# Casting the first key and query halves on the chip, with the mask built in two parts, in a block-sparse attention and feed-forward kernel

## The chip, the core and the metric

The kernel runs on one core of a Trainium2 chip. The metric is the device time of one execution in microseconds, as the median of several runs. The engines are TensorE (PE, matrix products; PEld is its weight load), VectorE (DVE), ScalarE (ACT), GpSimd (POOL) and SyncE (SP, which here only issues transfers). The transfers themselves are done by 16 DMA engines.

## The reference

Attention over 4 batches, 8 heads, 768 positions and 64 columns per head, in blocks of 32 positions. A query block sees its neighbours, the first and the last block, and three sampled blocks. The first and the last query block see everything. The result of all heads, 512 columns per position, goes through a normalisation and a feed-forward layer with 2048 hidden columns, and is added to what went in.

```python
scores = scale * np.matmul(q, k.transpose(0, 1, 3, 2))
mask = np.abs(blk_i - blk_j) <= window
mask = mask | (blk_i == 0) | (blk_j == 0) | (blk_i == n_blocks - 1) | (blk_j == n_blocks - 1)
for qb in range(n_blocks):
    for kb in sampled_blocks[qb]:
        mask[qb * block:(qb + 1) * block, kb * block:(kb + 1) * block] = True
scores = np.where(mask, scores, -1000000000.0)
attn = np.exp(scores - np.max(scores, axis=-1, keepdims=True))
attn = attn / (np.sum(attn, axis=-1, keepdims=True) + 1e-09)
x = np.matmul(attn, v)          # all heads side by side
xn = (x - mu) / np.sqrt(var + 1e-06) * g_ln
out = x + np.maximum(xn @ w_ch1, 0.0) @ w_ch2
```

## The kernel before

**Units, segments, slots.** A unit is a batch and a third of its positions (256 rows); there are 12. A unit has four segments, one for each pair of heads, and a segment four slots: two tiles of 128 rows by two heads, 192 slots in all. The first eight segments, two units, are called early.

**Split numbers.** Products of float32 numbers are made from float16 halves: for queries, keys, values and weights a high half is the cast of the number, and a low half the difference between the number and its high half. A score is three products, high by high, high by low and low by high (`scores`, L467 to L475), summed in a `ps` buffer. There are two such buffers, so the pair of slots that comes next needs the buffers of the pair before.

**A slot's way.** DVE reads the scores with the mask added and writes them with their maximum (`masked_max`, L478, L484). ACT takes the exponential (L498). In an early slot PE turns the result in 128x128 pieces with an identity matrix (L512), DVE and ACT copy the pieces out (L519), and PE multiplies with the values (`pa`, L588). Later slots write float16 halves (L549, L553) and are turned by a DMA on SP's queue (L559, L562). When a unit's four segments are done, `layer_norm` (L629) makes the normalised rows xh and xl (L731, L735), and `ffn` (L740) runs the two feed-forward products (L754, L835).

**Weights.** They arrive in 64 bits a number. Three DVE steps (L423, L427, L431), two ACT steps (L458, L460) and a POOL subtraction (L461) make float16 halves of each chunk: eight chunks of W1, sixteen of W2. This runs beside the first units' attention.

**Keys and queries before.** `loads_k` (L284) loads a float32 key by SP's queue (`raw`, L292; two buffers, each free when the low half has been made), and loads the same key a second time by POOL's queue with a cast to float16 on the way (`kh`, L299). The low half `kl` (L295) is made by DVE for the first key, by POOL for all others. `loads_q` (L305) does likewise for queries (`qr` L313, `qh` L317, `ql` L320).

**The mask.** `build_mask` (L254) makes `allow` from the host's fixed part and the sampled blocks: a conversion (L255), three compares (L259) with a maximum each (L262), and a scaling (L263), over all six tiles of 128 rows at once. The fixed part is fetched first, the sampled blocks second, both on ACT's queue (L235, L237).

**What sets the order.** All work is entered as tasks in a `Plan` (L26) with an engine, a cost, the tasks it comes after, a rank and the buffers it takes and gives. `run` (L92) steps through an assumed time: of the tasks that are ready it takes for each engine the one that could start first, or the lowest rank among near equals, and emits it. The result is a fixed order of instructions for each engine, which the engine works through in that order. Costs and due times only shape this order; on the chip an instruction waits for its data. The feed-forward matmuls have the rank 1e6: they fill PE's time when nothing else is ready. The mask has the rank -2000, and PE's tasks cost 1.9 times as much in the plan until it takes the array as warm.

## Time and profile before

| what | value |
|---|---|
| median of 3 runs | 816.51 us (814.61 to 822.39) |
| profiled execution, its time | 817.7 us |
| its span | 815.9 us |
| mean granted clock of PE | 0.987 |
| PE busy | 779.8 us, 96% |
| DVE busy | 610.9 us, 75% |
| ACT busy | 514.9 us, 63% |
| POOL busy | 173.9 us, 21% |

The span is what the profile covers; the time of the same execution is 1.8 us longer. A timeline row gives the start and the duration in us, the engine, the line, the operation with what it writes and reads, and in brackets how long the engine was idle before and what released it. A row of grouped instructions gives their count, the busy time, the mean duration in ns and the idle time in front of them. "SPq" and "ACTq" are the issuing of transfers; a landing is counted from the issue.

### The profile page before, as it was taken

To read this page: it belongs to the slowest core of one execution; us is meant where nothing else is said; L and a number is where in the kernel's file an instruction comes from. 1 tells how busy PE (TensorE), PEld (TensorE's weight loads), DVE (VectorE), ACT (ScalarE), POOL (GpSimd) and SP (SyncE) were. 2 spreads that over 40 slices of the span, in tenths; PEclk is the share of its full clock that TensorE was granted. 3 is DMA by queue.
4 is the path that set the end of the run, shared out by engine and by line. 5 is a ranking of instruction groups with operands and counts; after the bars stand their busy time and mean duration, and the time that the engine had idled before them with its cause. 6 is when DMAs were issued, how large, how long until landed. Compare 5 with 4: busy or idle time off the path is not lost.

```text
span 815.9 us, 18386 instructions
## 1 busy us (share of the span) xinstructions
PE 779.8 (96%) x7228; PEld 592.4 (73%) x7228; DVE 610.9 (75%) x1203; ACT 514.9 (63%) x942; POOL 173.9 (21%) x188
## 2 busy tenths in 40 slices
PE   4787899999999999999899999999999999999998
PEld 2454567777777867777677777777777777788887
DVE  5899988968988878868878778868869778745120
ACT  2778788668686666677666666668766656723020
POOL 4635454413211012143111012332100100000000
PEclk9799899999999999999999999999999999999999
DMA  9853424899989779999678699899697585750000
GB/s 283 289 174 95 132 70 116 159 159 207 168 155 141 130 136 168 160 193 173 124 136 141 107 152 174 168 181 169 131 144 142 107 150 101 115 107 2 27 2 27
DMA packets 293383, 112.49 MB, mean 138 GB/s; under 512 B 260400, under 2 KB 285104, under 8 KB 293296
## 3 DMA queue, kind: packets, MB, share of 16 engines
q1 hardware_dynamic: 283792, 104.91, 64.1%
q0 software_dynamic: 9216, 6.30, 6.2%
q8 instruction: 57, 0.93, 0.5%
q14 instruction: 30, 0.25, 0.1%
q10 hardware_dynamic: 288, 0.10, 0.1%
HBM read 48.34 MB, written 6.29 MB: 67 GB/s over the span
## 4 chain that ended last, share of the span: by engine, by line
PE 77%; DVE 11%; DMA 5%; ACT 4%; issue 1%; SPq 1%; ACTq 0%; DVEq 0%
PE bank L835 28%; PE bank L754 26%; PE ps L475 10%; PE pa L592 6%; DMA pt<-pl 3%; PE pa L597 3%; DVE p L484 2%; PE pa L588 2%; DVE pl L553 2%; PE bank L512 1%; ACT p L498 1%; DMA pt<-ph 1%; DVE w2h L427 1%; DMA samp_i<-sampled 1%; DMA raw<-w 1%
## 5 line engine op out<-in xcount | busy, mean ns | idle before, releaser
L498 ACT ACTIVATE p<-p,st 128x768 f32<-128x768 f32 x192 | 177.8, 926 | 43.4 <-DVE st L484 41.9
L549 ACT ACTIVATE ph<-p,st 128x768 f16<-128x768 f32 x160 | 145.3, 929 | 92.2 <-DVE st L540 42.0
L835 PE MATMUL bank<-hh,w2h 128*128 128x256 f16 x704 | 192.3, 273 | 2.5 <-DVE xc L685 2.5
L553 DVE SCALAR_TENSOR_TENSOR pl<-p,st,ph 128x768 f16<-128x768 f32 x160 | 164.3, 1038 | 38.9 <-DMA pt<-pl 37.4
L484 DVE CUSTOM_DVE_ANT_1 p<-ps,allow 128x768 f32<-128x768 f32 x192 | 178.4, 947 | 18.5 <-PE ps L475 17.4
L835 PE MATMUL bank<-hl,w2h 128*128 128x256 f16 x704 | 191.9, 273 | 0.0
L835 PE MATMUL bank<-hh,w2l 128*128 128x256 f16 x704 | 191.9, 273 | 0.0
L754 PEld LDWEIGHTS <-w1h 128*128 128x128 f16 x1536 | 146.9, 98 | 27.6 <-issue 10.7
L835 PEld LDWEIGHTS <-w2h 128*128 128x128 f16 x1408 | 134.5, 98 | 27.4 <-issue 12.4
L754 PE MATMUL bank<-xl,w1h 128*128 128x256 f16 x768 | 115.8, 274 | 0.0
L754 PE MATMUL bank<-xh,w1l 128*128 128x256 f16 x768 | 115.7, 273 | 0.0
L754 PE MATMUL bank<-xh,w1h 128*128 128x256 f16 x768 | 115.4, 273 | 0.1
L769 ACT ACTIVATE hh<-bank 128x512 f16<-128x512 f32 x96 | 56.6, 590 | 80.9 <-PE bank L754 80.2
L775 DVE SCALAR_TENSOR_TENSOR hl<-bank,hh 128x512 f16<-128x512 f32 x96 | 65.9, 686 | 35.4 <-ACT hh L769 35.1
L475 PE MATMUL ps<-kh,qh 64*128 64x256 f16 (+1 forms) x384 | 72.2, 338 | 14.2 <-DMA qh<-q 7.3
L592 PE MATMUL pa<-pt,vh 128*64 128x512 f16 x480 | 82.1, 383 | 0.7 <-issue 0.6
L754 PEld LDWEIGHTS <-w1l 128*128 128x128 f16 x768 | 73.9, 98 | 12.1 <-issue 3.8
L475 PEld LDWEIGHTS <-qh 64*128 64x128 f16 x768 | 32.5, 96 | 62.6 <-issue 28.2
L835 PEld LDWEIGHTS <-w2l 128*128 128x128 f16 x704 | 68.9, 98 | 8.0
L475 PE MATMUL ps<-kl,qh 64*128 64x256 f16 (+1 forms) x384 | 69.7, 334 | 1.4 <-DVE kl L295 1.4
L475 PE MATMUL ps<-kh,ql 64*128 64x256 f16 (+1 forms) x384 | 68.3, 334 | 1.2 <-DVE ql L320 1.2
L597 PE MATMUL pa<-pt,vl 128*64 128x256 f16 x480 | 67.4, 273 | 0.0
(106 smaller groups left out, 921.7 us busy)
## 6 DMA issues: line engine op xcount, KB each, us to landing
raw<-k SPq DMA_DIRECT2D x16, 384.0 KB, 4.6
qr<-q SPq DMA_DIRECT2D x48, 128.0 KB, 3.3
raw<-w SPq DMA_DIRECT2D x12, 512.0 KB, 3.6
out<-ot SPq DMA_DIRECT2D x48, 128.0 KB, 2.0
vr<-v SPq DMA_DIRECT2D x24, 192.0 KB, 2.9
w2l<-w SPq DMA_DIRECT2D x4, 1024.0 KB, 9.6
kh<-k POOLq DMA_DIRECT2D x16, 192.0 KB, 5.2
qh<-q POOLq DMA_DIRECT2D x48, 64.0 KB, 3.5
```

Of the source, the lines that this page charges most:

```text
L475: nc.tensor.matmul(s.ps[:, lo:hi], x[rows, s.qs], y[rows, lo:hi], start=n == 0, stop=n == len(terms) - 1)
L484: nc.vector.tensor_tensor_reduce(out=s.p.rearrange(blk, k=BLK), in0=s.ps[:, 0:S].rearrange(blk, k=BLK), in1=bias, scale=-0.125, scalar=3.0 ...
L498: nc.scalar.activation(s.p, s.p, AF.Exp, bias=s.st[:, j : j + 1], scale=-1.0, accum_out=total)
L549: nc.scalar.activation(s.ph, s.p, AF.Copy, scale=s.r)
L553: nc.vector.scalar_tensor_tensor(out=s.pl, in0=s.p, scalar=s.r, in1=s.ph, op0=ALU.mult, op1=ALU.subtract)
L588: nc.tensor.matmul(seg.pa[half[hh], 0:CH], vo.whole(hh)[:, t, :], pts[keys[hh]][:, t, :], start=t == 0, stop=t == KT - 1, skip_group_check ...
L592: nc.tensor.matmul(seg.pa[half[hh], 0 : 2 * CH], vo.vh[:, hh, t, :], pts[keys[hh]][:, t].rearrange("p i n -> p (i n)"), start=t == 0, stop ...
L597: nc.tensor.matmul(seg.pa[half[hh], 0:CH], vo.vl[:, hh, t, :], pts[keys[hh]][:, t, 0, :], start=False, stop=t == KT - 1, skip_group_check= ...
L754: nc.tensor.matmul(dst, w[:, ct, fs], x[:, ct, :], start=n == 0 and ct == 0, stop=n == 2 and ct == CT - 1, skip_group_check=True)
L769: nc.scalar.activation(u.hh[:, f : f + 2, :].rearrange("p f n -> p (f n)"), bank[plan.where("bank", own)], AF.Relu)
L775: nc.vector.scalar_tensor_tensor(out=u.hl[:, f : f + 2, :].rearrange("p f n -> p (f n)"), in0=bank[plan.where("bank", own)], scalar=0.0, i ...
L835: nc.tensor.matmul(dst, w[:, k, e * P : (e + 1) * P], x[:, k, :], start=k == 0 and n == 0, stop=k == FT - 1 and n == 2)
```

## The change

- **Casts.** The first four keys (`CASTK`) and the first four query loads (`CASTQ`) are no longer loaded a second time by POOL's queue. ACT casts the loaded float32 key or query; for the very first query DVE does. From the fifth on nothing changes.
- **Mask.** `build_mask(lo, hi)` makes the tiles from lo to hi. The first part has the two tiles of the first 256 positions (all that the first unit of a batch needs), the second the other four. A slot's maximum comes after its own part. Their ranks are 0 and 6, with 5400 and 12000 as the earliest planned times.
- **Fetch.** The sampled blocks are fetched ahead of the fixed part.
- **Planner.** The engines' planned times start at 700 and the transfers' at 1800 in place of 0. The array counts as warm when it was busy for over 0.85 of the last 3400 ns of planned time, and stays so down to 0.4. A `filler` of idle matmuls is defined, but called only for starts before `keep`, and `KEEP` is 0.

```diff
     def run(self):
-        clock = dict.fromkeys(("PE", "DVE", "ACT", "POOL", "SP"), 0.0)
+        clock = dict.fromkeys(("PE", "DVE", "ACT", "POOL", "SP"), 700.0)
-        bus, mode, done, warm, since = 0.0, None, 0, False, 0.0
+        bus, mode, done, warm = 1800.0, None, 0, False
...
-                    start = max([now] + [x.free if x.engine == "PE" == e or x.order == t.order
+                    start = max([t.wake] + [x.free if x.engine == "PE" == e or x.order == t.order
...
+            if t.engine == "PE" and start < self.keep:
+                self.fill(clock["PE"], start, 115 if warm else 220)
...
-                if start - clock["PE"] > self.idle:
-                    warm, since = False, start
-                warm = warm or start - since > self.heat
+                part = sum(max(0, b - max(a, start - self.span)) for a, b in self.work[-60:])
+                part /= self.span
+                warm = part > self.hot or warm and part > self.cold
...
+    KEEP = 0
+    CASTK, CASTQ = 4, 4
...
-    plan.idle, plan.heat, plan.deep = 2500.0, 4200.0, 7000.0
+    plan.span, plan.hot, plan.cold, plan.deep = 3400.0, 0.85, 0.4, 7000.0
+    plan.keep, plan.first = KEEP, 1400.0
...
-    nc.scalar.dma_start(allow, blocks)
     samp_i = const.tile([P, KT, 2 * NR], I32, name="samp_i")
     nc.scalar.dma_start(samp_i, sampled.bitcast(I32))
+    nc.scalar.dma_start(allow, blocks)
...
-    def build_mask():
-        nc.vector.tensor_copy(samp_f, samp_i.rearrange("p c (r t) -> p c r t", t=2)[:, :, :, 0])
+    def build_mask(lo, hi):
+        ts, n = slice(lo, hi), hi - lo
+        nc.vector.tensor_copy(samp_f[:, ts],
+                              samp_i.rearrange("p c (r t) -> p c r t", t=2)[:, ts, :, 0])
...
-        o.high = plan.add("POOL", 560, lambda: nc.gpsimd.dma_start(o.kh, ks[b, pr]), (o.raw,),
-                          rank, 2300, load=1100, order="k")
+        if idx < CASTK:
+            o.high = plan.add("ACT", 900, lambda: nc.scalar.copy(o.kh, o.kr), (o.raw,), rank)
+        else:
+            o.high = plan.add("POOL", 560, lambda: nc.gpsimd.dma_start(o.kh, ks[b, pr]),
+                              (o.raw,), rank, 2300, load=1100, order="k")
...
-        e, c = ("POOL", 660) if n else ("DVE", 650)
+        if n < CASTQ:
+            o.high = plan.add("ACT" if n else "DVE", 310 if n else 200, lambda: (
+                nc.scalar.copy if n else nc.vector.tensor_copy)(o.qh, o.qr), (o.raw,), rank)
...
+        e, c = ("POOL", 660) if n else ("DVE", 350)
...
-    mask = plan.add("DVE", 2300, build_mask, (), -2000, 100)
-    mask.more = 4000
+    masks = [plan.add("DVE", 1250, lambda: build_mask(0, TS), (), 0, 100),
+             plan.add("DVE", 2100, lambda: build_mask(TS, KT), (), 6, 100)]
+    masks[0].wake, masks[1].wake = 5400.0, 12000.0
...
-                last_m = plan.add("DVE", 880, lambda s=s: masked_max(s), (sc, mask, last_m),
+                last_m = plan.add("DVE", 880, lambda s=s: masked_max(s), (sc, masks[u.c > 0], last_m),
```

The lines of the program move by 18 to 36 places: the masked maximum is L519 after the change, the W1 and W2 steps on DVE are L458, L462 and L466.

**DVE at the program's start, up to the second masked maximum** (L484, ISA; `qh`, `ql`, `kl` are halves of the first query and key, `allow` is the mask). Before, from the conversion of the sampled blocks on, the compares and maxima shown once:

```order
L255 CAST samp_f<-samp_i 128x18
L259 TENSOR_TENSOR w1h<-allow,samp_f 128x144
L262 TENSOR_TENSOR allow<-allow,w1h 128x144
...
L263 TENSOR_SCALAR allow<-allow 128x144
L295 TENSOR_TENSOR kl_138<-raw_119,kh_137 128x768
L320 TENSOR_TENSOR ql_121<-qr_142,qh_141 128x256
L484 ISA p_192,st_193<-ps_174,allow 128x768
```

After, the halves stand ahead of the mask, and the mask has 48 columns in place of 144; behind the second maximum come the three steps of the first W1 chunk, which stood behind the third before:

```order
L349 CAST qh_132<-qr_133 128x256
L355 TENSOR_TENSOR ql_121<-qr_133,qh_132 128x256
L323 TENSOR_TENSOR kl_130<-raw_119,kh_129 128x768
L281 CAST samp_f<-samp_i 128x6
L287 TENSOR_TENSOR w1h<-allow,samp_f 128x48
L290 TENSOR_TENSOR allow<-allow,w1h 128x48
...
L291 TENSOR_SCALAR allow<-allow 128x48
L519 ISA p_191,st_192<-ps_169,allow 128x768
...
L458 TENSOR_SCALAR w2h<-w1r_156 128x1024
L462 SCALAR_TENSOR_TENSOR w2h<-w1r_156,w2h 128x1024
```

**DVE further on, between the fourth and the fifth masked maximum** (p_257 is the fourth before, p_250 after; w1r is a W1 chunk as loaded, `nm` the sums of the exponentials). Before:

```order
L484 ISA p_257,st_223<-ps_203,allow 128x768
L484 ISA st_223 128x1
L423 TENSOR_SCALAR w2h<-w1r_172 128x1024
L427 SCALAR_TENSOR_TENSOR w2h<-w1r_172,w2h 128x1024
L919 TENSOR_SCALAR nm_199<-nm_199 128x4
L920 RECIPROCAL nm_199<-nm_199 128x4
L484 ISA p_290,st_291<-ps_265,allow 128x768
```

After, the second part of the mask stands here, and the sums and the second step of the chunk come behind the fifth maximum. Up to the instruction that writes the first unit's xl, the order after has 22 masked maxima in place of 23, 20 copies in place of 22, and one W2 step less:

```order
L519 ISA p_250,st_240<-ps_201,allow 128x768
L519 ISA st_240 128x1
L554 COPY pt_1_247<-bank_101 128x2x128
L458 TENSOR_SCALAR w2h<-w1r_159 128x1024
L281 CAST samp_f<-samp_i 128x12
L287 TENSOR_TENSOR w1h<-allow,samp_f 128x96
L290 TENSOR_TENSOR allow<-allow,w1h 128x96
...
L291 TENSOR_SCALAR allow<-allow 128x96
L519 ISA p_293,st_294<-ps_254,allow 128x768
```

**ACT at the program's start** (L498 and L533 are exponentials, L519 and L554 copies of turned pieces, L458 and L493, L460 and L495 the two steps of a W chunk). Before:

```order
L498 ACTIVATE p_192,nm_199<-p_192,st_193 128x768
L498 ACTIVATE p_197,nm_199<-p_197,st_193 128x768
L519 COPY pt_0_232<-bank_101 128x4x128
L498 ACTIVATE p_222,nm_199<-p_222,st_223 128x768
L519 COPY pt_1_240<-bank_103 128x4x128
```

After, four casts stand in front of the first exponential, and the cast of the third key (kh_183) stands ahead of the second step of the first W1 chunk and of the third exponential; that of the fourth key follows seven instructions later:

```order
L328 CAST kh_129<-raw_119 128x768
L328 CAST kh_135<-raw_120 128x768
L349 CAST qh_138<-qr_139 128x256
L349 CAST qh_141<-qr_142 128x256
L533 ACTIVATE p_191,nm_198<-p_191,st_192 128x768
L533 ACTIVATE p_196,nm_198<-p_196,st_192 128x768
L554 COPY pt_0_230<-bank_101 128x4x128
L493 ACTIVATE w2h<-w2h 128x1024
L554 COPY pt_1_247<-bank_103 128x4x128
L328 CAST kh_183<-raw_119 128x768
L495 CAST w1h<-w2h 128x4x256
L533 ACTIVATE p_239,nm_198<-p_239,st_240 128x768
```

On PE, 132 transposes of 128x128 stand ahead of the first feed-forward matmul in place of 138, and otherwise the same instructions; the 2304 + 2304 feed-forward matmuls and all other counts are as before. On POOL the eight casting loads are gone. SP issues the same loads; the value load that stood ahead of the first W1 chunk now stands further back.

More of the change, by code (lines that the diff above doesn't have):

```diff
@@ L36, in __init__ @@
     def __init__(self):
-        self.tasks, self.rings, self.sets = [], {}, {}
+        self.tasks, self.rings, self.sets, self.work = [], {}, {}, []
     def ring(self, name, size):
@@ L49, in add @@
                             after=[x for x in after if x is not None], end=None, left=0, next=[],
-                            order=order, slack=slack)
+                            order=order, slack=slack, wake=0.0)
         for x in t.after:
@@ L90, in where, with fill @@
         return (self.rings.get(name) or self.sets[name]).at[owner]
+    def fill(self, now, start, each):
+        free = self.sets["bank"].free
+        place = min((p for p in free if free[p] is not None), key=lambda p: free[p], default=None)
+        begin = max(now, self.first, free[place] if place is not None else start)
+        count = int((start - begin - 300) // each)
+        if count >= 4:
+            self.filler(place, count)
+            free[place] = begin + each * count + 200
+            self.work.append((begin, begin + each * count))
     def run(self):
-        clock = dict.fromkeys(("PE", "DVE", "ACT", "POOL", "SP"), 0.0)
+        clock = dict.fromkeys(("PE", "DVE", "ACT", "POOL", "SP"), 700.0)
         held = {"DVE": 0.0, "POOL": 0.0}
         ready = {e: [t for t in self.tasks if t.engine == e and not t.left] for e in clock}
-        bus, mode, done, warm, since = 0.0, None, 0, False, 0.0
+        bus, mode, done, warm = 1800.0, None, 0, False
         while done < len(self.tasks):
@@ L114, in run @@
                     key = (max(start, now + self.LOOK), t.rank, t.n)
+                    start = max(start, now)
                     if pick is None or key < pick[0]:
```

20 lines of the change are left out of this document (14 added, 6 removed).

## Prediction

> **What bounds the kernel now.** I read the page first, for the share of each engine, then a table by stage, then the opening row by row.
>
> ```profile
> PE 779.8 (96%) x7228; PEld 592.4 (73%) x7228; DVE 610.9 (75%) x1203; ACT 514.9 (63%) x942; POOL 173.9 (21%) x188
> ```
>
> TensorE (PE) is busy for 96% of the span. That is an average over two stages, which the table by stage parts; its columns are the stretch, its length, then the busy time of PE, PEld, DVE, ACT and POOL, the granted clock, the DMA share and GB/s.
>
> ```profile
> 0.00:12.30 12.30, 2.46 (x12) 0.81 (x13) 5.21 (x13) 1.28 (x1) 7.08 (x15) 1.00 0.92 245
> 12.30:92.40 80.10, 63.73 (x445) 38.67 (x445) 70.52 (x131) 59.74 (x110) 37.88 (x29) 0.89 0.61 195
> 92.40:190.00 97.60, 94.33 (x867) 70.78 (x866) 83.16 (x164) 74.72 (x142) 40.42 (x41) 0.98 0.63 136
> 190.00:815.90 625.90, 619.33 (x5909) 482.08 (x5906) 452.04 (x896) 379.12 (x690) 88.55 (x104) 1.00 0.73 129
> ```
>
> From 92.4 us on PE is idle for 3.3 + 6.6 us in 723: there its own work sets the end, and the feed-forward matmuls fill whatever the attention leaves open. Before 92.4 us they don't exist yet, since the first unit's normalised rows are not ready; there the busiest engine is VectorE (DVE), 70.5 of 80.1 us from its first masked maximum on. So the end is, to a good approximation, the moment of the first feed-forward matmul plus a fixed amount of PE work. These rows from the timeline show that moment:
>
> ```profile
> 91.82 0.87 PE L512 MATMUL bank<-ident,p 128*128 128x128 f32 x6 [2.99 <-ACT p L498]
> 92.40 1.23 DVE L735 TENSOR_TENSOR xl<-xc,xh 128x1024 f16<-128x1024 f32 x1 [0.33 <-ACT xh L731]
> 92.53 0.60 PE L754 MATMUL bank<-xh,w1h 128*128 128x256 f16 x4
> ```
>
> The change works on the opening, whose rows (start, duration, engine, line) are:
>
> ```profile
> 5.83 0.18 DVE L255 CAST samp_f<-samp_i 128x18 f32<-128x18 int32 x1 [4.68 <-DMA samp_i<-sampled]
> 8.10 0.23 DVE L263 TENSOR_SCALAR allow<-allow 128x144 f32<-128x144 f32 x1
> 8.25 0.95 DVE L295 TENSOR_TENSOR kl<-raw,kh 128x768 f16<-128x768 f32 x1
> 8.77 1.92 POOL L295 TENSOR_TENSOR kl<-raw,kh 128x768 f16<-128x768 f32 x1 [4.30 <-DMA kh<-k]
> 9.12 1.86 DVE L320 TENSOR_TENSOR ql<-qr,qh 128x256 f16<-128x256 f32 x1
> 12.31 0.96 DVE L484 CUSTOM_DVE_ANT_1 p<-ps,allow 128x768 f32<-128x768 f32 x1 [1.34 <-PE ps L475]
> 16.14 0.96 DVE L484 CUSTOM_DVE_ANT_1 p<-ps,allow 128x768 f32<-128x768 f32 x1 [1.98 <-PE ps L475]
> ```
>
> The reader is to see one chain: the sampled blocks land, the whole mask is built on DVE until 8.33, only then come the low halves kl and ql, then the last score matmuls, and the first masked maximum at 12.31. The query's low half takes 1.86 us, although the key's, three times as large, takes 0.95: it stands still until GpSimd (POOL) is done with its own subtraction at 10.69.
>
> **The opening after the change (term 1).** Both ends of the cost follow from landings and durations. The first two rows are the landings of the first and the second key load, issued at 0.75 and 1.66; the first query load, issued at 1.20, has a row like the first.
>
> ```profile
> DMA to landing us min/median/max: 3.5/3.5/3.5
> DMA to landing us min/median/max: 5.2/5.2/5.2
> ...
> L460 ACT CAST w1h<-w2h 128x1024 f16<-128x1024 f32 x8 | 8.4, 1048 | 0.2
> L731 ACT CAST xh<-xc 128x256 f16<-128x256 f32 x4 | 1.5, 403 | 0.0
> L259 DVE TENSOR_TENSOR w1h<-allow,samp_f 128x144 f32<-128x144 f32 x3 | 0.9, 308 | 0.1
> L295 POOL TENSOR_TENSOR kl<-raw,kh 128x768 f16<-128x768 f32 x3 | 5.2, 1730 | 4.3 <-DMA kh<-k 4.3
> L320 POOL TENSOR_TENSOR ql<-qr,qh 128x256 f16<-128x256 f32 x9 | 6.8, 758 | 5.2 <-PE bank L512 3.4 <-issue 1.8
> ```
>
> Between the two ScalarE casts lies 0.645 us for 768 elements, so a key cast of 768 takes about 0.83 us and a query cast 0.40. No row shows DVE's cast of 128x256 from on-chip memory; it lies between the 0.18 of 18 elements and 0.42, DVE's copy of as many elements below, and I take 0.3, since both ends differ by little. The key lands at 4.25, its cast ends at 5.1; the query lands at 4.7, its cast and low half (0.42, between 0.31 for 144 and 0.95 for 768) end at 5.4; kl then ends at 6.4. The mask's first part is 8 instructions. At most they cost the 0.34 us per step of the whole mask (2.7), at least the 0.18 of its smallest (1.4); with 48 columns in place of 144 I take 0.22 each, 1.8. The mask is then ready at 8.2. The scores are ready by then too: from the low halves to the maximum it took 12.31 - 10.98 = 1.33 before, plus 0.4 for the matmuls with kl, from 6.4 that is 8.1. So the free end is a first maximum at **8.2**, 4.1 earlier.
>
> The other end is a stall. POOL's kl for the second key starts when that key has landed (6.9, or earlier) and ScalarE has cast it, so between 6.5 and 7.7: in the middle of the mask's first part. If one mask step has to stand still for it, 1.73 to 1.92 us are lost; if POOL's two ql behind it catch a step each, 2 x 0.76 more; and the first maximum is at **11.4**. The trace has such stalls for a subtraction (the 1.86 above) and for the small scalar op here, which ends with POOL's:
>
> ```profile
> 23.07 2.81 POOL L461 TENSOR_TENSOR w1l<-w2h,w1h 128x1024 f16<-128x1024 f32 x1 [9.35 <-ACT w1h L460]
> 23.95 1.95 DVE L919 TENSOR_SCALAR nm<-nm 128x4 f32<-128x4 f32 x1
> ```
>
> It has none for the mask's steps, since POOL was idle from 4.5 to 8.8 while they ran. I take one long stall, as both stalls in sight are of one POOL instruction: 8.2 + 1.9 = 10.1, which is **2.2 us earlier** (bounds 0.9 to 4.1). [...]
>
> **The first W1 chunk in the gap (term 2).** DVE now idles 1.98 us before its third maximum, because the second pair of scores needs the buffers of the first two. After the change the three steps of the first W1 chunk stand in that gap, so up to 2.0 us are won, if the chunk has landed by 10.1 + 1.8 = 11.9. Before, it was issued at 6.21 and landed 8.4 later (first of the two below), at 14.6, behind these transfers:
>
> ```profile
> DMA to landing us min/median/max: 8.4/9.9/11.4
> ...
> q0 software_dynamic: 720, 0.59, 24.9%
> ...
> q0 software_dynamic: 506, 0.50, 16.8%
> ```
>
> The second row is POOL's queue over the first 14.6 us: its casting transfers took 24.9% of the 16 DMA engines' time, 3.6 us, and the DMA share of the stretch to 12.3 us is 0.92, so nearly nothing else could use idle engines. All of those are gone, and one value load of 192 KB moves behind the chunk. I estimate the landing at 14.6 - 3.6 = 11.0, in time; if the relief is nil, DVE waits and the 2.0 us aren't won. I take **2.0 us**.
>
> **The second mask part and what POOL does beside it (term 3).** Its 8 instructions of up to 96 columns cost about 0.27 each, 2.1 us (bounds 1.4 and 2.7), now in the midst of DVE's list. Ahead of the first unit's xl DVE has in return one masked maximum, two copies and one small W2 step less:
>
> ```profile
> L484 DVE CUSTOM_DVE_ANT_1 p<-ps,allow 128x768 f32<-128x768 f32 x25 | 23.3, 946 | 5.8 <-PE ps L475 5.2 <-PE bank L512 0.5
> L519 DVE COPY pt<-bank 128x256 f32<-128x256 f32 x24 | 9.8, 417 | 1.2 <-PE bank L512 1.2
> L423 DVE TENSOR_SCALAR raw<-raw 128x512 int32<-128x512 int32 x4 | 1.7, 419 | 0.0
> L461 POOL TENSOR_TENSOR w1l<-w2h,w1h 128x1024 f16<-128x1024 f32 x8 | 20.4, 2548 | 14.4 <-ACT w1h L460 14.1 <-DMA w2h<-w 0.2
> ```
>
> 0.95 + 0.83 + 0.42 = 2.2, so the list comes out 0.1 shorter. While the second part runs, POOL subtracts the third key (1.73) and the first W1 chunk (2.55). Free, they cost nothing; catching one step each, 4.3. One stall of 2.1 in the middle stands against the 1.8 that the small scalar op loses now: **0.2 us later** together (bounds 1.9 earlier to 2.4 later).
>
> **The rest.** The six transposes that PE no longer does before its first feed-forward matmul come after it, 0.87 us by the row at 91.82: **0.9 later**. ScalarE gets four key casts and three query casts, 4 x 0.83 + 3 x 0.40 = 4.5 us. It is idle from 2.95 to 13.32 now, which covers the first four of them; the other three fall into the stretch where it is busy for 59.7 of 80.1 us. POOL loses eight DMA issues, which nobody waits for after the opening. The filler matmuls are never emitted, as KEEP is 0. The planner's new clock rule and starting times move no work by themselves; they are in the orders that I counted.
>
> **Sum.** -2.2 - 2.0 + 0.2 + 0.9 = -3.1. The profiled execution has a span of 815.9 in a time of 817.7; it would become 814.6. The median of the three runs shown is 816.5, 1.2 below it, so I forecast **813.4**. Early ends together: -4.1 - 2.0 - 1.9 + 0.9 = -7.1, 809.4. Late ends: -0.9 + 0 + 2.4 + 0.9 = +2.4, 818.9.
>
> **Rivals.**
> *ScalarE held up by key loads (slower).* The casts of the third and fourth keys stand in ScalarE's list ahead of exponentials, W1 casts and copies for TensorE. Before, only POOL waited for these loads, and they were slow:
>
> ```profile
> raw<-k SPq DMA_DIRECT2D x1, 384.0 KB, 11.1
> ...
> raw<-k SPq DMA_DIRECT2D x1, 384.0 KB, 15.1
> ```
>
> Issued at 9.23 and 11.90, they landed at 20.3 and 27.0. ScalarE reaches the third cast some 6.5 us after the first maximum (two exponentials, two copies and a W1 step wait for their producers), at 16.6, and the fourth at about 23. At the old landings it would stand for 3.7 and 4.0 us, and the third and fourth exponentials behind it: +7.7 against -3.1 is 821. Against it speaks that the third load is issued from 6.5 on, when kl frees its buffer, and that POOL's queue took 3.6 us up to 14.6 and 16.8% after: I work out 20.3 - 2.7 - 3.6 = 14.0, and for the fourth 27.0 - 3.6 - 2.1 = 21.3. It decides if they land later than 16.6 and 23.
> *The lead is lost on the way to 92 us (no change).* Of the 9.6 us that DVE idles between 12.3 and 92.4, much is waiting on others:
>
> ```profile
> DVE xT L618 <- ACT xT L615: 5.3, 4, 2.0
> DVE p L484 <- PE ps L475: 5.2, 5, 2.0
> ```
>
> If later links (W1 chunks, ScalarE) are due at fixed times, DVE idles longer there and the first feed-forward matmul stays near 92.5: 816.5. Against it speaks that the DMA share of that stretch is only 0.61.
> *More than the opening is won.* If the new order also spares half of the other 7 us of idle (9.6 less the 2.0 counted) and the clock isn't halved when the feed-forward starts (the 0.60 us above for four matmuls stands beside 0.87 and 1.01 for the next fours, 0.7 lost), and no mask step stands still (the 1.9 taken in term 1), it is 813.4 - 3.5 - 0.7 - 1.9 = 807.3. Nothing in the rows speaks for the new handovers being better.
>
> **How the numbers follow.** The forecast has 0.60, ScalarE held up 0.15, the lost lead 0.15, the larger gain 0.10. A measurement of this kernel can tell about 1%, 8.2 us, from no change. Faster by more than that (below 808.3) needs the largest gain in nearly full, or the early ends together and more: 0.10. Slower (above 824.7) needs ScalarE held up longer than the old landings: 0.05. Within 1%: 0.85. The range runs from 808.0, where the larger gain begins, to 819.5, past the late ends; it leaves out the full price of the held ScalarE.
>
> **What would show it.** Right: first masked maximum between 8.2 and 11.4, the first W1 step directly behind the second maximum without waiting for its load, the first feed-forward matmul near 89, and PE busy as before after it. A mask step of about 2 us would show the stall. Wrong: ScalarE waiting for raw key loads before a cast; the first feed-forward matmul at 92 or later; or the idle time of PE after it grown by several us, which no term here contains.

## The result and the profile after

| | us |
|---|---|
| before, median of 12 runs | 817.08 (814.61 to 822.39) |
| after, median of 12 runs | 822.95 (820.53 to 826.34) |
| ratio | 1.0078, 95% interval 1.0058 to 1.0098 |
| profiled execution of after | 826.34, span 824.6, granted clock 0.988 |

The change makes the kernel slower by 0.6 to 1.0%. The forecast was 813.4 with a range to 819.5; it is wrong in sign and size. The profiled execution of after is 3.4 us above the median of its kernel; a second trace of the kernel has a span of 819.4, and both are used below.

The busy line of the page reads much as before, but for DVE, which has 12 us more:

```profile
PE 781.0 (95%) x7228; PEld 597.1 (72%) x7228; DVE 623.0 (76%) x1212; ACT 518.0 (63%) x949; POOL 167.8 (20%) x180
```

The opening in the timeline of after, DVE first. The columns are start, duration, engine, line, operation:

```profile
6.78 1.54 DVE L287 TENSOR_TENSOR w1h<-allow,samp_f 128x48 f32<-128x48 f32 x1
8.36 0.59 DVE L290 TENSOR_TENSOR allow<-allow,w1h 128x48 f32<-128x48 f32 x1
8.98 0.59 DVE L287 TENSOR_TENSOR w1h<-allow,samp_f 128x48 f32<-128x48 f32 x1
9.61 0.21 DVE L290 TENSOR_TENSOR allow<-allow,w1h 128x48 f32<-128x48 f32 x1
...
10.19 0.96 DVE L519 CUSTOM_DVE_ANT_1 p<-ps,allow 128x768 f32<-128x768 f32 x1
...
11.95 0.69 DVE L458 TENSOR_SCALAR w2h<-w1r 128x1024 int32<-128x1024 int32 x1
...
18.09 1.65 DVE L281 CAST samp_f<-samp_i 128x12 f32<-128x12 int32 x1
19.77 2.15 DVE L287 TENSOR_TENSOR w1h<-allow,samp_f 128x96 f32<-128x96 f32 x1
...
22.25 0.26 DVE L287 TENSOR_TENSOR w1h<-allow,samp_f 128x96 f32<-128x96 f32 x1
...
23.55 0.95 DVE L519 CUSTOM_DVE_ANT_1 p<-ps,allow 128x768 f32<-128x768 f32 x1
...
33.39 3.93 DVE L466 SCALAR_TENSOR_TENSOR w2h<-w2l,w2h 128x1024 int32<-128x1024 int32 x1
```

POOL in the same timeline:

```profile
6.62 1.64 POOL L323 TENSOR_TENSOR kl<-raw,kh 128x768 f16<-128x768 f32 x1 [5.31 <-ACT kh L328]
8.22 1.29 POOL L355 TENSOR_TENSOR ql<-qr,qh 128x256 f16<-128x256 f32 x2
18.07 1.64 POOL L323 TENSOR_TENSOR kl<-raw,kh 128x768 f16<-128x768 f32 x1 [8.56 <-ACT kh L328]
19.67 2.14 POOL L496 TENSOR_TENSOR w1l<-w2h,w1h 128x1024 f16<-128x1024 f32 x1
...
33.47 2.13 POOL L496 TENSOR_TENSOR w1l<-w2h,w1h 128x1024 f16<-128x1024 f32 x1
35.55 0.67 POOL L355 TENSOR_TENSOR ql<-qr,qh 128x256 f16<-128x256 f32 x1
```

The two lists have to be read side by side. The first masked maximum stands at 10.19, near the forecast of 10.1, but not by the one long stall that was taken for it: three mask steps stand still, one for each of POOL's three instructions, kl and two ql. They take 1.54, 0.59 and 0.59 where a step takes 0.21, so 1.3 + 0.4 + 0.4 = 2.1 us are lost. The first W1 step stands directly behind the second maximum, as forecast. Then comes the second mask part, and it takes from 18.09 to 23.6, 5.5 us, where 2.1 and one stall were counted. Its conversion lasts 1.65 and ends at 19.74, when POOL's kl ends (19.71); its first compare lasts 2.15 and ends at 21.92, when POOL's w1l ends (21.81). The same compare a moment later takes 0.26. A further stall stands at 33.39: a W1 step that takes 1.22 elsewhere takes 3.93, behind two POOL instructions in a row.

PE is idle for part of the meantime. In the timeline of PE, the transposes that need the fifth exponential, and the first feed-forward matmul:

```profile
25.62 1.06 PE L547 MATMUL bank<-ident,p 128*128 128x128 f32 x6 [3.88 <-ACT p L533]
92.95 0.64 PE L789 MATMUL bank<-xh,w1h 128*128 128x256 f16 x3
```

It waits for 3.88 us ahead of them, and the first feed-forward matmul comes at 92.95, not near 89. The table by stage from the first masked maximum to that moment, for before and then for after (columns as in the prediction):

```profile
12.31:92.53 80.22, 63.85 (x446) 38.80 (x446) 70.65 (x132) 59.88 (x110) 37.87 (x29) 0.89 0.61 195
```

```profile
10.19:92.95 82.76, 60.84 (x441) 38.53 (x441) 74.93 (x132) 58.99 (x107) 36.39 (x26) 0.92 0.54 179
```

DVE is idle for 9.6 us of that stretch before and for 7.8 after: the gap of 2.0 is gone, as forecast. But it is busy for 74.9 us instead of 70.7. With the instructions that moved (2.2 less, 2.1 more) and one stall of 2.1 in place of 1.8 it should have been 70.9. The 4.1 us are the second stall of the mask part (3.4 lost in it instead of 2.1, 1.3 more) and the W1 step (2.7 of its 3.93), together 4.0. Two smaller differences about cancel in this sum: two more W2 steps (0.69 each) stand behind the first feed-forward matmul, and the stalls of under 1 us, most of them behind 40 us, add up to some 2 us more than before (each DVE row less the usual length of its kind).

### The profile page after: what moved, and what is told of

Same layout as the page of the kernel before. It is cut to its first block, busy times and chain, and to the rows that moved or that the text cites. A ratio compares the mean times of both kernels' runs of the same rounds, so it can differ in the third digit from the quotient of the medians.

```text
span 824.6 us, 18394 instructions
## 1 busy us (share of the span) xinstructions
PE 781.0 (95%) x7228; PEld 597.1 (72%) x7228; DVE 623.0 (76%) x1212; ACT 518.0 (63%) x949; POOL 167.8 (20%) x180
## 4 chain that ended last, share of the span: by engine, by line
PE 55%; DMA 9%; DVE 7%; ACT 6%; issue 2%; SPq 1%; POOL 0%; ACTq 0%; POOLq 0%; DVEq 0%
PE bank L789 21%; PE bank L870 21%; PE ps L510 6%; PE pa L627 5%; DMA pt<-pl 3%; DMA pt<-ph 3%; ACT ph L584 2%; DVE pl L588 2%; PE pa L632 2%; ACT p L533 2%; DMA vr<-v 2%; DVE p L519 1%; DVE xc L756 0%; ACT vr L366 0%; DVE ot L826 0%
## 5 line engine op out<-in xcount | busy, mean ns | idle before, releaser
L533 ACT ACTIVATE p<-p,st 128x768 f32<-128x768 f32 x192 | 177.9, 927 | 39.4 <-DVE st L519 37.5
L588 DVE SCALAR_TENSOR_TENSOR pl<-p,st,ph 128x768 f16<-128x768 f32 x160 | 168.0, 1061 | 32.8 <-DMA pt<-pl 28.9
L519 DVE CUSTOM_DVE_ANT_1 p<-ps,allow 128x768 f32<-128x768 f32 x192 | 178.5, 948 | 15.7 <-PE ps L510 15.1
L789 PE MATMUL bank<-xh,w1h 128*128 128x256 f16 x768 | 117.2, 274 | 1.5 <-ACT xh L766 1.4
L510 PE MATMUL ps<-kh,qh 64*128 64x256 f16 (+1 forms) x384 | 69.1, 335 | 14.0 <-DVE st L519 9.0
L632 PE MATMUL pa<-pt,vl 128*64 128x256 f16 x480 | 69.3, 273 | 0.0
L510 PE MATMUL ps<-kl,qh 64*128 64x256 f16 (+1 forms) x384 | 67.1, 330 | 0.7 <-DVE kl L323 0.7
L510 PE MATMUL ps<-kh,ql 64*128 64x256 f16 (+1 forms) x384 | 66.3, 330 | 0.0
```

Of the source, the lines that this page charges most:

```text
L510: nc.tensor.matmul(s.ps[:, lo:hi], x[rows, s.qs], y[rows, lo:hi], start=n == 0, stop=n == len(terms) - 1)
L519: nc.vector.tensor_tensor_reduce(out=s.p.rearrange(blk, k=BLK), in0=s.ps[:, 0:S].rearrange(blk, k=BLK), in1=bias, scale=-0.125, scalar=3.0 ...
L533: nc.scalar.activation(s.p, s.p, AF.Exp, bias=s.st[:, j : j + 1], scale=-1.0, accum_out=total)
L588: nc.vector.scalar_tensor_tensor(out=s.pl, in0=s.p, scalar=s.r, in1=s.ph, op0=ALU.mult, op1=ALU.subtract)
L632: nc.tensor.matmul(seg.pa[half[hh], 0:CH], vo.vl[:, hh, t, :], pts[keys[hh]][:, t, 0, :], start=False, stop=t == KT - 1, skip_group_check= ...
L789: nc.tensor.matmul(dst, w[:, ct, fs], x[:, ct, :], start=n == 0 and ct == 0, stop=n == 2 and ct == CT - 1, skip_group_check=True)
```

## The experiments

One table first. "First matmul" is the start of the first feed-forward matmul in the trace, "behind it" the span less that. "Left over" is the time difference less the shift of the first matmul against 91.3 (the second trace of the kernel before) and less the 0.9 of the six transposes where these stand behind it (the change, e4, e7, e8, e10 and e11); where there are two traces of a changed kernel, their mean is used. e3 has none, since its list ahead of the first matmul holds twelve score matmuls more. The time difference is the ratio less 1, times 816.

| kernel | first matmul | behind it | median us | ratio, interval | left over |
|---|---|---|---|---|---|
| before, first / second trace | 92.5 / 91.3 | 723.4 / 726.9 | | | |
| change, first / second trace | 93.0 / 93.3 | 731.7 / 726.1 | 822.95 | 1.0078, 1.0058 to 1.0098 | 3.6 |
| e1 opening, old order | 90.9 | 723.8 | 816.57 | 1.0000, 0.9974 to 1.0025 | 0.4 |
| e2 casts, old order | 92.9 | 722.1 | 818.53 | 1.0037, 1.0016 to 1.0058 | 1.4 |
| e3 planner alone | 94.0 | 729.5 | 825.87 | 1.0118, 1.0089 to 1.0147 | |
| e4 change, casting loads | 95.5 | 724.9 | 822.27 | 1.0086, 1.0053 to 1.0118 | 1.9 |
| e5 change, old planner (two traces) | 92.7 / 95.4 | 724.7 / 725.2 | 821.63 | 1.0071, 1.0045 to 1.0097 | 3.0 |
| e6 before, LOOK 110 | 92.1 | 726.2 | 819.27 | 1.0037, 1.0007 to 1.0067 | 2.2 |
| e7 before, new clock rule | 89.2 | 726.8 | 820.14 | 1.0053, 1.0027 to 1.0078 | 5.5 |
| e8 change, whole mask first | 90.0 | 725.7 | 817.47 | 1.0024, 0.9999 to 1.0048 | 2.4 |
| e9 = e5, whole mask first (two traces) | 88.2 / 87.5 | 724.3 / 724.7 | 815.78 | 1.0002, 0.9974 to 1.0030 | 3.6 |
| e10 change, second part early | 92.0 | 724.4 | 820.19 | 1.0059, 1.0032 to 1.0086 | 3.2 |
| e11 change, second part twice | 95.0 | 725.7 | 824.62 | 1.0096, 1.0063 to 1.0129 | 3.2 |
| e12 = e1, mask in two parts | 93.5 | 725.3 | 819.59 | 1.0039, 1.0014 to 1.0064 | 1.0 |

### The parts of the change, each alone

**e1.** The opening in the planned order of before: the first two keys and three queries cast on the chip, the sampled blocks fetched first, the whole mask behind ql.

```diff
...
-lambda: nc.gpsimd.dma_start(o.kh, ks[b, pr])
+lambda: nc.scalar.copy(o.kh, o.kr) if idx < 2 else nc.gpsimd.dma_start(o.kh, ks[b, pr])
...
+        def low():
+            (nc.gpsimd if n else nc.vector).tensor_sub(o.ql, o.qr, o.qh)
+            if n == 0:
+                build_mask()
...
-    mask = plan.add("DVE", 2300, build_mask, (), -2000, 100)
+    mask = plan.add("DVE", 2300, lambda: None, (), -2000, 100)
```

> The kernel before with its whole planned order kept; only the opening is changed: the first two keys and first three queries are cast on ScalarE and VectorE, the sampled blocks are fetched first, and the whole mask is built behind the first low halves. Theory A (the loss of 0.8% comes from the new order of the instructions, in which TensorE waits more often between 33 and 250 us): the opening by itself is a gain or nothing, first masked maximum between 10 and 12 us, time 813.5 to 817.5. Theory B (the loss comes from the moved work itself, casts on ScalarE and mask steps that stand still behind GpSimd): 819 or more.

816.57, ratio 1.0000: no gain and no loss shows, within 2 us either way. The opening itself isn't what made the change slower, and the gain that the forecast gave it doesn't show.

**e2.** The casts alone, in the order of before: four keys and four queries, by the emitted instruction only.

```diff
-lambda: nc.gpsimd.dma_start(o.kh, ks[b, pr])
+lambda: nc.scalar.copy(o.kh, o.kr) if idx < 4 else nc.gpsimd.dma_start(o.kh, ks[b, pr])
...
-lambda: nc.gpsimd.dma_start(o.qh, qs[u.b, pr, u.c])
+lambda: nc.scalar.copy(o.qh, o.qr) if n < 4 else nc.gpsimd.dma_start(o.qh, qs[u.b, pr, u.c])
```

> The kernel before with its planned order kept and the mask untouched; the casts of the first four keys and queries stand on ScalarE at the places where GpSimd issued the casting loads. Theory A: within 2.5 us of the kernel before, 814.5 to 819.5. Theory B: ScalarE is held up by key loads or its 4.5 us of casts delay the exponentials: 820 or more, with ScalarE waiting on raw key loads for over 2 us.

818.53, ratio 1.0037. The interval lies above 1, so the casts cost something in that order, about 3 us. The trace, of this kernel's fastest execution (816.78), shows ScalarE held up: the casts of the third and the fourth key wait for their loads, and DVE then waits for the exponential behind them. Two rows of the timeline of ACT and one of DVE:

```profile
15.46 0.83 ACT L299 CAST kh<-raw 128x768 f16<-128x768 f32 x1 [1.44 <-DMA raw<-k]
21.89 0.83 ACT L299 CAST kh<-raw 128x768 f16<-128x768 f32 x1 [2.57 <-DMA raw<-k]
...
26.02 0.96 DVE L919 TENSOR_SCALAR nm<-nm 128x4 f32<-128x4 f32 x1 [3.38 <-ACT p L498]
```

The fifth masked maximum comes at 27.11, against 23.70 in the second trace of before, 1.1 of it from a later first maximum (11.08 against 9.99). That is a rival of the prediction at work, in another order than that of the change.

**e3.** The planner's new starting times and clock rule alone, on the kernel before.

```diff
-        clock = dict.fromkeys(("PE", "DVE", "ACT", "POOL", "SP"), 0.0)
+        clock = dict.fromkeys(("PE", "DVE", "ACT", "POOL", "SP"), 700.0)
...
-        bus, mode, done, warm, since = 0.0, None, 0, False, 0.0
+        bus, mode, done, warm = 1800.0, None, 0, False
...
-                warm = warm or start - since > self.heat
+                warm = part > self.hot or warm and part > self.cold
```

> The kernel before with the planner's new starting times (700 and 1800) and its new rule for a warm array, all instructions the same, so only their order differs. Theory A: the order moves the time by several us, 820 to 825 if the planner's new rule is what costs. Theory B: 815.5 to 818.5.

825.87, ratio 1.0118: slower than the change as a whole. No instruction is added or taken away here; the numbers only put the same work into another order. Which waits cost it these 9.6 us isn't shown.

**e4.** The change with its own order held, but the first halves, of keys and of queries, still cast by POOL's transfers; the lines shown are those of the keys.

```diff
-            o.high = plan.add("ACT", 900, lambda: nc.scalar.copy(o.kh, o.kr), (o.raw,), rank)
+            o.high = plan.add("ACT", 900, lambda: nc.gpsimd.dma_start(o.kh, ks[b, pr]), (o.raw,), rank)
```

> The changed kernel with its planned order kept; the first four keys and queries are loaded a second time by GpSimd's queue with a cast, as before, in place of the casts on ScalarE and VectorE. Theory A: the order still costs, 822 to 827 (the opening is late again by about 2 us). Theory B: without the casts on ScalarE it comes back to 816 to 819.

822.27, ratio 1.0086, as the change. The run doesn't price the casts alone, since the first halves come late again: the first masked maximum stands at 13.15 instead of 10.19. From there to the first feed-forward matmul it takes 82.4 us, against 82.8 and 83.2 in the two traces of the change, so in that stretch the casts on ACT cost nothing that can be seen.

### Is it the planner's new order?

After e3 and e4 the planner was the first suspect.

**e5.** The change with the old starting times and the old clock rule (the edit of e3 undone). The order of PE then differs from that of before in 81 of 13702 lines; the new clock rule alone (e7) changes 3763.

> The changed kernel with its casts and its mask in two parts, but the planner's old starting times and old rule for a warm array; the order it plans differs from the order before in only 81 lines of 13702 on TensorE. Theory A (the planner's rule and times, by the order they give, are what costs): 813 to 818, no loss against before. Theory B (casts and mask parts cost by themselves): 820 or more.

821.63, ratio 1.0071. The loss stays when the planner's part is undone, so this theory fell. The trace has the same second mask part, in the timeline of DVE:

```profile
17.91 1.61 DVE L281 CAST samp_f<-samp_i 128x12 f32<-128x12 int32 x1
19.56 2.15 DVE L287 TENSOR_TENSOR w1h<-allow,samp_f 128x96 f32<-128x96 f32 x1
...
23.32 0.95 DVE L519 CUSTOM_DVE_ANT_1 p<-ps,allow 128x768 f32<-128x768 f32 x1
```

**e6 and e7.** Two orders as a measure of scatter: the kernel before with the planner looking less far ahead, and with the new clock rule alone.

```diff
-    LOOK = 120
+    LOOK = 110
```

```diff
-                if start - clock["PE"] > self.idle:
-                    warm, since = False, start
-                warm = warm or start - since > self.heat
+                part = sum(max(0, b - max(a, start - self.span)) for a, b in self.work[-60:])
+                part /= self.span
+                warm = part > self.hot or warm and part > self.cold
```

> The kernel before with the planner's tie window LOOK at 110 in place of 120, which has no meaning for the chip and changes 3442 lines of the order on TensorE. Theory A1 (the new warm rule itself makes worse orders): as before, 814.5 to 818.5. Theory A2 (the order before is an unusually good one and any other order of this planner loses several us): 819 to 827.

> The kernel before with the new rule for a warm array alone, starting times as before; 3763 lines of the order on TensorE change. Theory A1: 821 to 827, like the planner's changes together (825.9). Theory A2: anything from 817 to 827, no closer to 825.9 than the kernel with LOOK 110.

819.27 (1.0037) and 820.14 (1.0053). Both are slower than before, though they do the same work, and e7 even has its first feed-forward matmul at 89.2. A new order can cost 3 to 4 us by itself; where it loses them isn't shown, as the 726.2 and 726.8 us behind that moment are no more than the 726.9 of before's second trace.

**e8.** The change, order held; the whole mask is built where the first part stands, and nothing where the second stood.

```diff
-    masks = [plan.add("DVE", 1250, lambda: build_mask(0, TS), (), 0, 100),
-             plan.add("DVE", 2100, lambda: build_mask(TS, KT), (), 6, 100)]
+    masks = [plan.add("DVE", 1250, lambda: build_mask(0, KT), (), 0, 100),
+             plan.add("DVE", 2100, lambda: None, (), 6, 100)]
```

> The changed kernel with its order kept, but all six tiles of the mask are built in the first part and nothing stands at the second part's place; the first part grows by about 0.8 us, and 5.5 us of mask steps and their standing still at 18 to 23.6 us go. If that stall is a cost that reaches the end: 3 us or more below the changed kernel, 817 to 820. If the later waits of the order set the end whatever happens at 20 us: within 1.5 us of it, 821.5 to 824.5.

817.47, ratio 1.0024: 0.54% below the change, with the first feed-forward matmul at 90.0 instead of 93.0. This points to the second mask part at its place, and the next four runs test that. Not all of its stalls are gone: in the timeline of DVE a W1 step at 24.94 takes 2.33 instead of 1.22, beside POOL's kl, and a scalar op at 22.27 takes 1.10 instead of 0.16, beside w1l.

### The second mask part

**e9.** The edit of e8 on the kernel of e5. PE, ACT and POOL have the same instructions in the same order as in e5; DVE's list differs by the mask alone.

> The change with the planner's old starting times and old clock rule (the kernel that had ratio 1.0071), its order held, but the mask built whole in the first part's place and nothing at the second part's place. Theory (the second mask part, 5.5 us of DVE at its place of which 3.4 us stand still beside POOL, reaches the end): first masked maximum 0.6 to 0.9 us later than in that kernel, the fifth some 3 us earlier, time 816 to 817.5 us, ratio 1.000 to 1.002. Rival (any new order costs 0.4 to 0.5%, and the low time of the run with the whole mask in the change's own order was chance): no difference that can be seen, 820 to 822 us, ratio 1.005 to 1.008.

815.78, ratio 1.0002, against 1.0071 for e5; the intervals lie apart. The timeline of DVE up to the fifth masked maximum, and PE's first feed-forward matmul:

```profile
10.79 0.96 DVE L519 CUSTOM_DVE_ANT_1 p<-ps,allow 128x768 f32<-128x768 f32 x1
...
18.99 0.96 DVE L519 CUSTOM_DVE_ANT_1 p<-ps,allow 128x768 f32<-128x768 f32 x1 [0.20 <-PE ps L510]
...
88.17 0.60 PE L789 MATMUL bank<-xh,w1h 128*128 128x256 f16 x4
```

The first maximum is 1.0 later than in e5 (9.77), the fifth 4.3 earlier, and the first feed-forward matmul 4.5 earlier. The table by stage from the first maximum to that matmul, for e5 and for e9:

```profile
9.77:92.70 82.93, 62.09 (x447) 38.35 (x447) 76.20 (x140) 61.95 (x113) 35.10 (x27) 0.92 0.56 182
```

```profile
10.79:88.17 77.38, 61.33 (x447) 38.13 (x447) 70.74 (x132) 61.62 (x113) 35.02 (x26) 0.93 0.59 189
```

Eight DVE instructions are gone, 5.46 us of DVE's time, and the stretch is 5.55 shorter, at nearly the same granted clock (0.92 and 0.93). In this pair of traces DVE's time sets the end one for one, and the time of the kernel follows (5.6 us by the two ratios). The second traces of the two kernels:

```profile
10.20:95.39 85.19, 66.41 (x447) 40.28 (x447) 75.71 (x140) 61.70 (x113) 35.42 (x26) 0.88 0.54 175
```

```profile
10.82:87.51 76.69, 59.76 (x446) 37.30 (x446) 70.41 (x132) 61.50 (x113) 35.63 (x26) 0.96 0.60 192
```

Here DVE has 5.30 us less and the stretch is 8.50 shorter. The other 3.2 are idle time of DVE, which go with the granted clock: 0.88 against 0.96. So these two agree that the part's time reaches the end, but they don't show the one for one.

**e10.** The change, order held, the second part directly behind the second masked maximum, where POOL has no work.

```diff
-             plan.add("DVE", 2100, lambda: build_mask(TS, KT), (), 6, 100)]
+             plan.add("DVE", 2100, lambda: None, (), 6, 100)]
...
+        if s.i == 1:
+            build_mask(TS, KT)
```

> The change, order of everything else held; only the eight instructions of the second mask part stand directly behind the second masked maximum, where POOL has no work (its stretch from 9.5 to 18.1 us), and their old place is empty. Theory (the stalls beside POOL are what costs): the part takes 2.1 us instead of 5.5, no step of it over 0.3 us, the third maximum is 2.1 us later, the fifth 1 to 3 us earlier, time 817.5 to 819 us, ratio 1.002 to 1.004. Rival 1 (a second part costs wherever it stands, since DVE carries the opening): 820 to 822. Rival 2 (order scatter): 822 to 823, ratio 1.007 to 1.009, as the change itself.

820.19, ratio 1.0059: above the expected 1.002 to 1.004, and in time the first rival's number. The part behaves as expected, 2.1 us without a stall, from 12.14 to 14.22 in the timeline of DVE:

```profile
12.14 0.17 DVE L281 CAST samp_f<-samp_i 128x12 f32<-128x12 int32 x1
12.34 0.26 DVE L287 TENSOR_TENSOR w1h<-allow,samp_f 128x96 f32<-128x96 f32 x1
...
14.22 0.69 DVE L458 TENSOR_SCALAR w2h<-w1r 128x1024 int32<-128x1024 int32 x1
...
25.63 2.69 DVE L466 SCALAR_TENSOR_TENSOR w2h<-w1r,w2h 128x1024 int32<-128x1024 int32 x1
32.39 3.03 DVE L466 SCALAR_TENSOR_TENSOR w2h<-w2l,w2h 128x1024 int32<-128x1024 int32 x1
```

But POOL's kl at 25.60 now meets a W1 step, which takes 2.69 instead of 1.22. So a part of the stalls only changed its victim: DVE's busy time from the first masked maximum to the first feed-forward matmul is 73.5, against 74.9 in the change and 70.7 in e8. The expectation had left that out. It also points to a cost of the 2.1 us of the part's own steps where no stall is: e10's first matmul is 2.0 later than e8's, which single traces alone don't carry, and the intervals of the two ratios overlap.

**e11.** The change, order held, the six compare and maximum steps of the second part issued twice.

```diff
-        for r in range(NR):
+        for r in list(range(NR)) * (2 if lo else 1):
```

> The change, order held; the six compare and max steps of the second mask part are issued twice in the same place (the result is the same). Theory (DVE's time at that place reaches the end one for one): the six added steps take 0.26 us and a gap of 0.03 each, 1.8 us together, more if one of them stands still beside POOL; time 824 to 826 us, ratio 1.010 to 1.012. Rival (DVE's time there is absorbed by later waits, and the order costs the time): as the change, 822 to 823.5, ratio 1.007 to 1.009.

824.62, ratio 1.0096. The fifth maximum comes at 25.34, 1.8 and 1.0 later than in the two traces of the change, the first feed-forward matmul at 95.00, 1.7 to 2.0 later, and the ratio is 0.18% higher (1.5 us), as the theory said. The intervals of the two ratios overlap, so neither the times nor single traces show this by themselves; they agree with it.

**e12.** The kernel of e1 with the mask in two parts, the second ahead of the fifth masked maximum.

```diff
-                build_mask()
+                build_mask(0, TS)
...
+        if s.i == 4:
+            build_mask(TS, KT)
```

> The first run (the opening alone in the order of before, ratio 1.0000) with the mask in two parts: the first behind ql, the second directly ahead of the fifth masked maximum, beside POOL's subtraction of the third key; everything else in the order of before. Theory: the first part is 0.8 us shorter, the second takes 2.1 us and one stall of about 1.6 us beside POOL, so DVE has 2.9 us more ahead of the first feed-forward matmul; time 818.5 to 820, ratio 1.003 to 1.005. Rival (the lead and the loss of the opening are both absorbed on the way): 816 to 817, ratio 0.999 to 1.001.

819.59, ratio 1.0039, against 1.0000 for e1. So the split seems to cost in the order of before too, though the two intervals still overlap (1.0014 to 1.0025). Its rows, in the timelines of DVE and PE:

```profile
22.04 1.95 DVE L929 TENSOR_SCALAR nm<-nm 128x4 f32<-128x4 f32 x1
24.11 1.47 DVE L256 CAST samp_f<-samp_i 128x12 f32<-128x12 int32 x1
25.62 0.26 DVE L262 TENSOR_TENSOR w1h<-allow,samp_f 128x96 f32<-128x96 f32 x1
...
93.48 0.60 PE L764 MATMUL bank<-xh,w1h 128*128 128x256 f16 x4
```

One stall of 1.3 (1.47 less 0.17) and the part's own steps stand here; the scalar op of 1.95 stands in e1 and before as well. The first feed-forward matmul comes 2.6 later than in e1, the time is 3.2 us longer by the ratios.

### How far one trace carries

**f1 to f4.** The change, the kernel before, e5 and e9, each traced a second time, since the 731.7 us behind the first feed-forward matmul stood alone in the table.

> The changed kernel, traced a second time. If the long stretch behind the first feed-forward matmul (731.7 us) belongs to the order, it is 729 us or more again; if it belongs to that execution, it is 724 to 727. In both cases the second mask part takes 5 to 6 us and the first feed-forward matmul stands at 92.5 to 93.5.

> The kernel before, traced a second time. If the moment of the first feed-forward matmul is set by the order, it stands at 92.0 to 93.0 again and the rest takes 722 to 725 us; if it varies between executions by more than 1 us, differences of that size between traces of two kernels say nothing.

> The change with the old planner, traced a second time: first feed-forward matmul at 92.2 to 93.2 and 723 to 726 us behind it, if both belong to the order; the stalls of the second mask part again 1.6 and 2.1 us.

> The same with the whole mask in the first part's place, traced a second time: first feed-forward matmul at 87.5 to 89, if the order sets it. Behind it 724 us as in its first trace would make a time near 814; 727 us or more would show that this order gives the lead back behind that moment, as its median of 815.78 suggests.

The change has 726.1 this time: 5.5 of the 731.7 belonged to that execution. The stalls are the same (1.61 and 2.14). The first feed-forward matmul moves by 0.4, 1.2, 2.7 and 0.7 us between two traces of one kernel; e5's and that of before miss the ranges expected for them. Differences between single traces count here only above some 3 us. For e5 the 2.7 are idle time of DVE (9.5 us instead of 6.7 between the first maximum and that matmul), in the trace with the lower granted clock (0.88 instead of 0.92); that the clock is the cause isn't shown.

The second trace of before showed something that no theory had. Its opening, in the timeline of DVE:

```profile
4.88 0.17 DVE L255 CAST samp_f<-samp_i 128x18 f32<-128x18 int32 x1 [3.72 <-DMA samp_i<-sampled]
7.29 0.95 DVE L295 TENSOR_TENSOR kl<-raw,kh 128x768 f16<-128x768 f32 x1
8.16 0.42 DVE L320 TENSOR_TENSOR ql<-qr,qh 128x256 f16<-128x256 f32 x1
9.99 0.96 DVE L484 CUSTOM_DVE_ANT_1 p<-ps,allow 128x768 f32<-128x768 f32 x1 [1.41 <-PE ps L475]
```

The sampled blocks land 0.95 us earlier than in the trace of the prediction. DVE's ql is done (8.58) before POOL's kl begins (8.83), the stall of 1.86 isn't there, and the first masked maximum stands at 9.99 instead of 12.31. The other three kernels with that opening, e3, e6 and e7, have it at 10.20, 10.18 and 10.52. Four executions out of five have no such stall.

## Why the prediction was wrong, point by point

**The end is the first feed-forward matmul plus a fixed amount: right, but only within some 2.4 us either way.** Behind it lie 722.1 to 726.9 us in 16 of 18 traces; the two others are 729.5 and 731.7. That scatter is as large as the forecast gain.

**Term 1, first maximum 2.2 us earlier: right in the number by luck, wrong in what it was measured against.** 10.19 and 10.07 in the two traces, 10.1 forecast. The free end of 8.2 was right (10.19 less the 2.1 lost is 8.1). But the stall of 1.9 that was chosen is the sum of three shorter ones, 1.3 and twice 0.4: each POOL instruction caught a mask step, as in the late end, and each cost less than its whole length, so that 2.1 were lost and not the late end's 3.2. The 12.31 that it was taken from is one execution's, and the other four of that opening stand at 9.99 to 10.52. Against these the term is worth nothing, which fits e1's ratio of 1.0000. The prediction named the stall of 1.86, but not that it hung on 0.35 us between POOL's start (8.77) and DVE's (9.12).

**Term 2, the W1 chunk in the gap, 2.0: right up to the first feed-forward matmul.** The step stands at 11.95 without a wait, and DVE's idle time fell by 1.8.

**Term 3, the second mask part and POOL beside it, +0.2: this is the step that failed.** Its late end (+2.4) had two stalls in the mask part, and two came, 3.4 us instead of the one of 2.1 that was taken; the W1 step behind w1l and ql lost 2.7 more, which no term held. Together 4.0, so +4.2 in place of +0.2. e5 against e9 prices the part at its place at 5.5 us of DVE's time and 5.6 us of the kernel's, and the change against e8 at 4.4 us of the kernel's; in both pairs the intervals lie apart. e12 agrees in another order, and e10 and e11 agree that stalls and own steps both count. The count of what DVE has less was made up to xl, but the first feed-forward matmul needs only xh: two more W2 steps stand behind it, 1.4 us, which small stalls took back.

**The rest.** The four key casts cost 0.83 each on ACT and wait for no load once the opening is over; in the timeline of ACT the third and the fourth:

```profile
17.15 0.84 ACT L328 CAST kh<-raw 128x768 f16<-128x768 f32 x1
25.94 0.83 ACT L328 CAST kh<-raw 128x768 f16<-128x768 f32 x1
```

So the rival of ScalarE held up fell for the change; in e2, where the third cast stands at 15.46, it shows. The rival of the lost lead has nearly the right time for the first matmul and the wrong reason: DVE doesn't idle longer on the way, it is busier. "The planner's new clock rule and starting times move no work by themselves; they are in the orders that I counted" failed as well, since I counted orders only up to the first feed-forward matmul: the rule alone costs 0.53% (e7), and both together 1.18% (e3). In the change they add nothing that the runs can tell (1.0078 with, 1.0071 without).

**Does it add up?** From the first matmul of before in its second trace, 91.3: 0 for the opening, 2.0 less for the gap, 4.2 more for term 3 make 93.5; the two traces have 92.95 and 93.31 (their measured shift, 1.8, is used here). With the 0.9 of the transposes that is 2.7 us of the 6.4 that the ratio gives. Some 3.6 are left over, with an uncertainty of about 2 from single traces. The table shows what they go with: e1, e2 and e12, in the order of before, have 0.4 to 1.4 left over, all others 1.9 to 5.5. That a new order loses a few us behind the first feed-forward matmul would fit, but e5 and e9, with 3.0 and 3.6, differ from before in only 81 lines on PE, and the gap between the groups is smaller than the uncertainty. This cause stays open. Of the 9.5 us between the forecast of -3.1 and the 6.4, term 3 holds 4.0 and the 2.2 of term 1 against an untypical opening make 6.2; some 3.3 are unexplained. Not explained either is that e9, with the first matmul 3.4 earlier, is no faster than before (2.1 faster to 2.4 slower by the interval), although its two traced executions, 814.3 and 813.95, have most of the lead in their time. It is the best version of the change that was run, and it doesn't beat the kernel before.

## What to carry to other kernels

Before work is put into the list of an engine that carries a stage, look at what its neighbour does at that moment. Here each of POOL's three subtractions beside the opening of after, and both beside its second mask part, held one mask step of DVE, for 0.4 to 1.9 us and never as long as the subtraction itself (0.7 to 2.1). Moving the work to a quiet place helped only as far as the neighbour's instructions didn't meet the next step instead (in e10 a W1 step took 2.69 in place of 1.22). A stall in the one trace that hangs on a few tenths of a us between two engines may not be there in the next execution: the query's low half took 1.86 in the first trace of before and 0.42 in the second. So price a gain from it at a part, or look at a second trace first. A change that reorders a planned program is to be compared with a reordering that does nothing, which here cost 0.4 to 1.2% (e6, e7, e3).

## What the runs showed of the hardware

**Several kinds of DVE operations stood still here until the POOL subtraction beside them ended.** In after, a conversion of 12 numbers a row took 1.65 us beside POOL's kl and ended 0.03 after it; without POOL beside it, it took 0.17 (e10). A compare of 96 took 2.15 beside w1l and ended 0.11 after it, against 0.26 without. In before, a scalar op of 4 numbers took 1.95 beside w1l and ended 0.02 after it; in after, with POOL idle, it took 0.16. Which property of an operation makes it stand still isn't shown. In the opening of after one mask step stood still for each of the three POOL instructions (1.54, 0.59 and 0.59 in place of 0.21), and the first maximum came at 10.19 and not at the late end of 11.4, because each lost less than was priced. The masked maximum shows no such stall: its 192 take 0.93 to 0.96 each in the first traces of before and after, beside POOL or not. One in before, and the POOL instruction beside it, both of their usual length:

```profile
26.03 0.93 DVE L484 CUSTOM_DVE_ANT_1 p<-ps,allow 128x768 f32<-128x768 f32 x1
...
25.84 1.63 POOL L295 TENSOR_TENSOR kl<-raw,kh 128x768 f16<-128x768 f32 x1
```

**Between two POOL instructions in a row the waiting DVE step was not always let in.** In after, the W1 step of 33.39 waited for w1l and then for ql, which ran for its usual 0.67, and ended 1.1 after it, at 37.32. Its row begins 0.08 before w1l's (33.47), so here it wasn't the earlier row that went through first. In e10 the step of 25.63 was let in when kl ended at 27.24, and POOL's next instruction, a ql, stood still instead, with 1.64 in place of 0.67, as the timeline of POOL shows:

```profile
25.60 1.64 POOL L323 TENSOR_TENSOR kl<-raw,kh 128x768 f16<-128x768 f32 x1 [0.93 <-ACT kh L328]
27.21 1.64 POOL L355 TENSOR_TENSOR ql<-qr,qh 128x256 f16<-128x256 f32 x1
```

What decides between the two isn't known from these runs.
